# Eight instead of ten token blocks of MLP1 in front of the attention loop, and thirteen instead of seven MLP2 blocks in five stretches

## The chip, the cores and the metric

The kernel runs on one core of a Trainium2 chip. The metric is device time of one execution in microseconds (us), as the median of several runs. TensorE (PE) does the matrix products, VectorE (DVE), ScalarE (ACT) and GpSimd (POOL) the elementwise work, and SyncE (SP) issues nearly all DMA transfers.

## What is computed

The reference mixes two branches over S = 2048 tokens of D = 640 channels with a gate for each token. Branch A is attention with 32 query heads of 20 channels and a single key and value head. Branch B is the token-mixing MLP of an MLP-Mixer: layer norm over channels, then two products along the token axis (2048 to F = 1728 and back) with a tanh-approximated gelu between them.

```python
g = _sigmoid((x * gate_w).sum(-1, keepdims=True))
a = _A_ref(x, A_wq, A_wk, A_wv, A_wo)
b = _B_ref(x, B_w1, B_b1, B_w2, B_b2)
return g * a + (1 - g) * b
...
scores = jnp.einsum("bhqd,bkd->bhqk", q, k) * (Dh ** -0.5)
p = _softmax(scores, axis=-1)
o = jnp.einsum("bhqk,bkd->bhqd", p, v)
...
h = _layernorm(x, axis=-1)
u = jnp.einsum("bsd,sf->bdf", h, w1) + b1
u = _gelu(u)
y = jnp.einsum("bdf,fs->bds", u, w2) + b2
```

All inputs are float32. The kernel keeps that accuracy by splitting numbers into a high and a low part and summing three products: high by high, high by low, low by high.

## The kernel before

**Stages.** The order of the instructions on every engine is written out by hand (a manual schedule). There are five stages: (1) layer norm, transposes and the q, k, v projections; (2) a stage in front of the loop, in which TensorE computes blocks of MLP1 and starts on the row maxima; (3) the attention loop of 326 stretches, in which the rest of MLP1, all of MLP2 and part of the output projection are filled in between the scores; (4) a tail with the last attention units and output projections; (5) the last stores.

**Row tiles.** The score products contract over at most 62 rows, so two of them fit into the TensorE array one above the other. Each MLP product is cut into halves of 64 rows, and one half can run beside a score product in the other rows. In the loop, a stretch `k` works its scores in the rows of `b = k % 2` and its MLP matmuls in the other rows.

**Attention units.** There are 32 items (four query blocks of 512 by eight groups of four heads) of 16 key blocks, thus 512 units. A unit needs four score matmuls (L660), four exponentials (ScalarE, L663) and four matmuls with v (L687). The row maximum of the scores must be known before the exponentials, so all scores are computed once more, in another layout (L479), and reduced on VectorE (`tensor_reduce`, L482): 64 matmuls and reduces an item, 2048 in all. Of them, `LEAD = 48` pairs are done in stage 2, by `lead()`; the loop does six a stretch on average.

**MLP1.** A block is 128 of the 1728 hidden tokens for one half (320) of the channels; there are 14 blocks for each of two halves, 28 in all. A block has 16 steps of six matmuls: three products by two row halves. `PRO` of them, all of the first channel half, stand in stage 2 (L589), where both row halves run side by side into two banks, `pu0` and `pu1`. `pop_chain()` is called after each step and takes the next entry of the list `chain`, which holds the gelu of the block before: add the two banks (`add`, L525, VectorE), square (ScalarE), `cube` (L529, VectorE), `tanh` (ScalarE), `prod` (L535, VectorE), `high` (ScalarE), `low` (L541, GpSimd); `None` entries leave steps out. `cube_p`, `prod_p` (L548, L549) and `high_p` are the same on GpSimd, in two instructions each; the last block in front and the loop's blocks use them. In the loop a block takes six stretches of 16 matmuls.

**Lead.** In stage 2, the pairs of row-max matmuls are spread evenly over the steps from the fourth to the sixth before last. The matmuls take three PSUM banks in turn (`ps_m`), and a bank is free again when its reduce is done.

**Weights.** `w1_upto(n)` makes the high and low part of weight chunks up to chunk n: the high part (`wh`) on ScalarE for the first `4 * PRO` chunks and on GpSimd after that (L128), the low part (`wl`, L129) always on GpSimd. A block needs four chunks. SP's queue loads 256 KB for each, four chunks ahead.

**Query parts.** While `one_by_one` is set, the six transfers of a query tile are queued in `q_parts_due` and issued one at each quarter of a block, so that they don't crowd the weight loads. The queue must be empty before `fetch_max(0)` near the end of the stage.

**MLP2.** For each of 16 token blocks `st` and each channel half there are 81 matmuls of 64 rows. A block takes six stretches a channel half (13 or 14 matmuls each), or five (16 or 17). Five are possible because `twin_u` copies the first two hidden blocks to the other 64 rows, which evens out the two row halves over an odd number of stretches. `FIVE`, the number of blocks with five, is computed so that the loop has 326 stretches:

```python
FIVE = 6 * NS - (163 - 3 * (2 * FC - PRO) - 2 * NA)
```

With NS = 16, FC = 14, NA = 10 and PRO = 10 this is 7.

**A stretch.** `main(k, vs)` merges two lists by assumed times: the scores and row maxima in one row half, the MLP matmuls (and one or two row maxima) in the other. With more than 15 MLP matmuls it takes the pattern MANY (six scores, six row maxima), otherwise one of FEW (six scores with seven or five row maxima in turn). At the end of the MLP matmuls stands `signal()`, a tiny VectorE memset of `flag` (L673), so that a profile shows one `flag` for each stretch.

Of the kernel before, what the change touches and what calls it, by code (L numbers as in the profile page):

```python
# [12 lines left out]
ALU = mybir.AluOpType  # L13
# [12 lines left out]
NQB = S // NB  # L26
NQ = H // 4
NU = NQB * NQ
PRO = 10
LEAD = 48  # L30
TAIL = 24
BLOCKS = (2,) * 12
# [7 lines left out]
def mix_kernel(ctx: ExitStack, tc: tile.TileContext, A_x, A_wq, A_wk, A_wv, A_wo,  # L40
               B_x, B_w1, B_b1, B_w2, B_b2, gate_w, out):
    nc = tc.nc
# [3 lines left out]
    def f32(ap):  # L46
        return ap.bitcast(F32)
# [70 lines left out]
    def w1_upto(n):  # L118
        while fetched[0] < min(n, len(chunks)):
            c = fetched[0]  # L120
            w1_load(c + 1)
            wr = w1raw[c]
            wh = w1p.tile([P, HS, P], F32R, name="wh")
            wl = w1p.tile([P, HS, P], F32R, name="wl")
            if c < 4 * PRO:
                nc.scalar.activation(wh, wr, AF.Copy)  # L126
            else:
                nc.gpsimd.tensor_copy(wh, wr)  # L128
            nc.gpsimd.tensor_sub(wl, wr, f32(wh))  # L129
            w1t[c] = wh, wl  # L130
            fetched[0] += 1
            w1_load(c + 4)
# [20 lines left out]
    one_by_one, q_parts_due = [False], []  # L153

    def new_q(n):
        if n < NU:
            qtiles[n] = load_q(n, "qst")
# [309 lines left out]
    def ms_next(b):  # L467
        k = given[b]
        if k >= 32 * NU:
            return None  # L470
        given[b] += 1
        n, r = divmod(k, 32)
        (kq, pr), qt = divmod(r // 4, 2), r % 4

        def step():
            if n not in mtiles:
                mtiles[n] = mpool.tile([P, 16, 4], F32, name="mp")
            ms = next_bank()
            nc.tensor.matmul(ms, qmax[n][64 * b:64 * b + 60, pr, qt * P:(qt + 1) * P],  # L479
                             kst[64 * b:64 * b + 60, kq * NB:(kq + 1) * NB], start=True, stop=True)  # L480
            c = (2 * b + pr) * 4 + qt
            nc.vector.tensor_reduce(mtiles[n][:, c, kq:kq + 1], ms, axis=AX.X, op=ALU.max)  # L482
            issued[b] += 1
            if min(issued) == 32 * n + 1:
                new_qmax(n + 1)

        return step

    def ms_done():
        n = len(row_max)  # L490
        if n < NU and min(issued) >= 32 * (n + 1):
            mm = mmpool.tile([P, 16], F32, name="mm")
            nc.vector.tensor_reduce(mm, mtiles.pop(n), axis=AX.X, op=ALU.max)
            mn = mmpool.tile([P, 2, 16], F32R, name="mn")
            nc.gpsimd.tensor_scalar(mm, mm, -1.0, None, op0=ALU.mult)
            nc.gpsimd.tensor_copy(mn[:, 0, :], mm)
            nc.gpsimd.tensor_sub(mn[:, 1, :], mm, f32(mn[:, 0, :]))
            row_max[n] = mn

    def store_max(n):  # L500
        mn = row_max[n]
        mt = mpool.tile([P, 32], F32, name="mt")
        nc.vector.transpose(mt, f32(mn).rearrange("p j c -> p (j c)"))
        nc.sync.dma_start(out=m_scr[n], in_=mt)

    def fetch_max(n):
        src = m_scr[n].rearrange("(i j b r) e -> j b r i e", j=2, b=2, r=8)
        for b in range(2):
            for j in range(2):
                rows = f32(qtiles[n][64 * b + 60 + j:64 * b + 61 + j])  # L510
                nc.sync.dma_start(out=rows.rearrange("o p (t i e) -> o (p t) i e", i=4, e=32), in_=src[j, b][None])

    chain = []

    def gelu(d, fc, accs):
        both = fin.tile([P, D], F32, name="yo")
        xg, t1 = both[:, :HD2], both[:, HD2:]
        hi, lo = u_hi[d][:, fc, :], u_lo[d][:, fc, :]
        nc.scalar.activation(xg, accs[0][:, :HD2], AF.Identity, bias=bias[:, NS + fc:NS + fc + 1])

        def square():
            nc.scalar.activation(t1, xg, AF.Square)

        def add():
            nc.vector.tensor_add(xg, xg, accs[1][:, :HD2])  # L525
            square()

        def cube():
            nc.vector.scalar_tensor_tensor(t1, t1, 1.0 / 0.044715, xg, op0=ALU.add, op1=ALU.mult)  # L529

        def tanh():
            nc.scalar.activation(t1, t1, AF.Tanh, scale=GC * 0.044715)

        def prod():
            nc.vector.scalar_tensor_tensor(t1, t1, 1.0, xg, op0=ALU.add, op1=ALU.mult)  # L535

        def high():
            nc.scalar.activation(hi, t1, AF.Copy)

        def low():  # L540
            nc.gpsimd.tensor_sub(lo, t1, f32(hi))  # L541

        def cube_p():
            nc.gpsimd.tensor_scalar(t1, t1, 1.0, 1.0 / 0.044715, op0=ALU.mult, op1=ALU.add)
            nc.gpsimd.tensor_mul(t1, t1, xg)

        def prod_p():
            nc.gpsimd.tensor_scalar(t1, t1, 1.0, 1.0, op0=ALU.mult, op1=ALU.add)  # L548
            nc.gpsimd.tensor_mul(t1, t1, xg)  # L549

        def high_p():
            nc.gpsimd.tensor_copy(hi, t1)
            nc.gpsimd.tensor_sub(lo, t1, f32(hi))

        if len(accs) == 2 and fc == PRO - 1:
            add()
            chain.extend((cube_p, None, tanh, prod_p, high_p))
        elif len(accs) == 2:
            chain.extend((None, None, add, None, None, cube, tanh, None, prod, high, None, low))
        else:  # L560
            chain.extend((square, cube_p, None, tanh, prod_p, high_p))

    def pop_chain():
        f = chain.pop(0) if chain else None
        if f:
            f()

    with tc.tile_pool(name="psb", bufs=2, space=PSUM, side="right") as psb:
        at, skip, last = 0, 3, NS * PRO - 6
        one_by_one[0] = True  # L570

        def lead():
            for b in range(2):
                ms_next(b)()
            ms_done()

        for fc in range(PRO):
            pu = [psb.tile([P, NB], F32, name=f"pu{r}") for r in range(2)]
            for hf in range(4):
                w1_upto(4 * fc + hf + 4)  # L580
                if fc and q_parts_due:
                    q_parts_due.pop(0)()
                wh, wl = w1t.pop(4 * fc + hf)
                for c in range(HS):
                    st = hf * HS + c
                    for k, (w, h) in enumerate(((wh, h_hi[0]), (wh, h_lo[0]), (wl, h_hi[0]))):
                        for r in range(2):
                            rows = slice(64 * r, 64 * r + 64)
                            nc.tensor.matmul(pu[r][:, :HD2], w[rows, c, :], h[rows, st, :],  # L589
                                             start=(st == 0 and k == 0), stop=(st == NS - 1 and k == 2))  # L590
                    done = [max(0, min(x, last) - skip) * LEAD // (last - skip) for x in (at, at + 1)]
                    if done[1] > done[0]:
                        lead()
                    at += 1
                    pop_chain()
                if fc == 1 and hf == 0:
                    new_q(0)
                if fc == PRO - 2 and hf == 2:
                    assert not q_parts_due
                    one_by_one[0] = False  # L600
                    fetch_max(0)
            gelu(0, fc, pu)
            if fc == PRO - 3:
                store_max(0)
# [198 lines left out]
    def room(i):  # L803
        t, at = (u0, slot[0])[i % 8 // 4], 3 * D * (i % 4)
        return (t[:, at:at + 2 * D].rearrange("p (j c q) -> p j c q", j=2, q=P), f32(t[:, at + 2 * D:at + 3 * D]))
# [303 lines left out]
    for c in range(CUT // P, DC):  # L1109
        r = min(P, HEAD - c * P)  # L1110
        for st in held:
            oT, _ = room(len(jobs) - 4 + st - (NS - 4))
# [12 lines left out]
    for i in range(4):  # L1125
        st = NS - 4 + i
        for d in range(2):
# [7 lines left out]
            if (i, d) in ((0, 0), (1, 0), (2, 1), (3, 0), (3, 1)):  # L1135
                nc.vector.scalar_tensor_tensor(at[:, :HD2], acc[:, :HD2], g_col[:, st:st + 1], parts[st][:, sl],
                                               op0=ALU.mult, op1=ALU.add)
# [29 lines left out]
```

## Time and profile before

| what | us |
|---|---|
| median of 3 runs | 1677.76 (1677.33 to 1678.45) |
| profiled execution, its own time | 1677.69 |
| its span, first to last instruction | 1675.9 |
| first matmul of the blocks in front of the loop (L589) | at 96.1 |
| last matmul of these blocks | at 179.8 |
| first flag of the loop | at 183.2 |
| last flag of the loop | at 1596.4 |

The granted TensorE clock is 1.000 for the span. The stages differ in what keeps each engine busy:

| stretch of the span | length | DVE busy | ACT busy | POOL busy |
|---|---|---|---|---|
| MLP1 in the loop, 210 to 650 | 440 | 398.18 | 336.06 | 226.50 |
| MLP2 in five stretches, 650 to 957 | 307 | 276.79 | 224.69 | 82.68 |
| MLP2 in six stretches, 957 to 1423 | 466 | 418.85 | 346.03 | 105.58 |
| output projection, 1423 to 1597 | 174 | 156.81 | 133.69 | 33.35 |
| tail, 1597 to 1676 | 79 | 25.43 | 48.96 | 5.59 |

How to read the rows quoted below. A row of a group or line gives line, engine, operation, tiles written and read, count, and times in us, with durations of one instruction in ns. A row in order of time has its start, its length, and in square brackets how long the engine sat idle before it and whose work ended that; several instructions of a kind that follow each other closely are one row with their count. TensorE counts as busy almost everywhere, since matmuls overlap in the pipeline, so its pace is read from the starts of matmuls and not from its busy time.

### The profile page before, as it was taken

To read this page: it belongs to the slowest core of one execution; us is meant where nothing else is said; L and a number is where in the kernel's file an instruction comes from. 1 tells how busy PE (TensorE), PEld (TensorE's weight loads), DVE (VectorE), ACT (ScalarE), POOL (GpSimd) and SP (SyncE) were. 2 spreads that over 40 slices of the span, in tenths; PEclk is the share of its full clock that TensorE was granted. 3 is DMA by queue.
4 is the path that set the end of the run, shared out by engine and by line. 5 is a ranking of instruction groups with operands and counts; after the bars stand their busy time and mean duration, and the time that the engine had idled before them with its cause. 6 is when DMAs were issued, how large, how long until landed. Compare 5 with 4: busy or idle time off the path is not lost.

```text
span 1675.9 us, 38869 instructions
## 1 busy us (share of the span) xinstructions
PE 1668.3 (100%) x14865; PEld 1102.7 (66%) x14865; DVE 1440.1 (86%) x2745; ACT 1193.4 (71%) x2356; POOL 588.4 (35%) x727
## 2 busy tenths in 40 slices
PE   9999999999999999999999999999999999999998
PEld 7899766666666666666666656656665655666665
DVE  6679889989999998898989899899899989988933
ACT  4444677777777777777777777777777777777775
POOL 6568555555555543222323222122122220112210
PEclk9999999999999999999999999999999999999999
DMA  7665322222232321223212212122121221333611
GB/s 210 204 179 148 88 70 73 75 77 73 64 76 60 85 68 48 67 74 81 66 57 67 70 49 66 42 67 61 40 78 56 59 60 38 103 107 110 192 51 40
DMA packets 178304, 138.20 MB, mean 82 GB/s; under 512 B 33305, under 2 KB 144054, under 8 KB 178118
## 3 DMA queue, kind: packets, MB, share of 16 engines
q1 hardware_dynamic: 177830, 135.39, 29.3%
q8 instruction: 117, 1.92, 0.5%
q14 instruction: 69, 0.57, 0.1%
q10 hardware_dynamic: 288, 0.33, 0.1%
HBM read 102.36 MB, written 31.65 MB: 80 GB/s over the span
## 4 chain that ended last, share of the span: by engine, by line
PE 95%; issue 2%; DVE 1%; SPq 1%; ACT 0%; DMA 0%; POOL 0%; POOLq 0%; DVEq 0%; ACTq 0%
PE o L687 28%; PE ms L479 15%; PE s L660 12%; PE g L753 10%; PE ms L660 7%; PE g L932 6%; PE s L479 5%; PE pp L298 4%; PE pu L589 3%; PE g L878 2%; DVE mp L482 1%; PE ms L834 0%; PE pt L290 0%; ACT p L663 0%; SPq L195 0%
## 5 line engine op out<-in xcount | busy, mean ns | idle before, releaser
L482 DVE TENSOR_REDUCE mp<-ms 128x1 f32<-128x512 f32 x1298 | 839.3, 685 | 122.3 <-PE ms L479 97.8
L663 ACT ACTIVATE p<-s 128x512 f32<-128x512 f32 x1296 | 714.8, 607 | 241.0 <-PE s L660 205.5
L479 PE MATMUL ms<-kst,qmx 60*128 60x512 f32 x1298 | 552.4, 433 | 0.7 <-DVE mp L482 0.5
L660 PE MATMUL s<-qst,kst 62*128 62x512 f32 x1296 | 524.3, 410 | 0.0
L482 DVE TENSOR_REDUCE mp<-s 128x1 f32<-128x512 f32 x750 | 493.2, 682 | 23.3 <-PE s L479 23.0
L687 PE MATMUL o<-p,v_sb 128*32 128x512 f32 x4096 | 511.4, 601 | 0.0
L663 ACT ACTIVATE p<-ms 128x512 f32<-128x512 f32 x752 | 420.7, 602 | 112.3 <-PE ms L660 96.5
L479 PEld LDWEIGHTS ms<-kst,qmx 60*128 60x128 f32 x1298 | 238.3, 185 | 181.4 <-ACT p L663 91.3
L479 PE MATMUL s<-kst,qmx 60*128 60x512 f32 x750 | 311.8, 429 | 0.4 <-DVE yo L525 0.4
L660 PE MATMUL ms<-qst,kst 62*128 62x512 f32 x752 | 308.6, 410 | 0.0
L660 PEld LDWEIGHTS s<-qst,kst 62*128 62x128 f32 x1296 | 238.0, 186 | 92.4 <-DVE flag L673 62.0
L932 PE MATMUL g<-slot,wh 64*128 64x320 f32 x1152 | 268.0, 312 | 0.0
L129 POOL TENSOR_TENSOR wl<-wr,wh 128x512 fp32r<-128x512 f32 x176 | 230.5, 1312 | 42.9 <-ACT wh L126 21.7
L687 PEld LDWEIGHTS o<-p,v_sb 128*32 128x32 f32 x4096 | 97.6, 109 | 184.7 <-issue 176.9
L753 PE MATMUL g<-slot,wh 64*128 64x320 f32 x864 | 205.1, 313 | 0.0
L753 PE MATMUL g<-u,wh 64*128 64x320 f32 x864 | 205.0, 313 | 0.0
L932 PEld LDWEIGHTS g<-slot,wh 64*128 64x128 f32 x1152 | 190.7, 184 | 2.0 <-issue 1.7
L660 PEld LDWEIGHTS ms<-qst,kst 62*128 62x128 f32 x752 | 139.3, 185 | 66.1 <-issue 44.4
L932 PE MATMUL g<-slot,wl 64*128 64x320 f32 x576 | 179.9, 312 | 0.0
L709 POOL TENSOR_TENSOR ot<-ot,rl 128x512 f32<-128x512 f32 x30 | 31.5, 1051 | 361.0 <-DVE rl L708 361.0
L128 POOL CAST wh<-wr 128x512 fp32r<-128x512 f32 x136 | 83.4, 613 | 187.6 <-PE g L753 67.4
L753 PEld LDWEIGHTS g<-slot,wh 64*128 64x128 f32 x864 | 145.1, 184 | 2.4 <-ACT yo L761 2.1
(203 smaller groups left out, 2210.1 us busy)
## 6 DMA issues: line engine op xcount, KB each, us to landing
wr<-in_B_w_dram SPq DMA_DIRECT2D x152, 256.0 KB
qmx<-q_scr SPq DMA_DIRECT2D x192, 80.0 KB
qst<-q_scr SPq DMA_DIRECT2D x192, 80.0 KB
slot<-o_scr SPq DMA_DIRECT2D x20, 320.0 KB
y_scr<-yo SPq DMA_DIRECT2D x16, 320.0 KB
o_scr<-oh SPq DMA_DIRECT2D x124, 40.0 KB
o_scr<-ol SPq DMA_DIRECT2D x124, 40.0 KB
q_scr<-qh SPq DMA_DIRECT2D x19, 256.0 KB
```

The lines of the kernel that those rows point to most:

```text
L128: nc.gpsimd.tensor_copy(wh, wr)
L129: nc.gpsimd.tensor_sub(wl, wr, f32(wh))
L298: nc.tensor.matmul(pp, w, t, start=first and n == 0, stop=not more and n == len(steps) - 1)
L479: nc.tensor.matmul(ms, qmax[n][64 * b:64 * b + 60, pr, qt * P:(qt + 1) * P], kst[64 * b:64 * b + 60, kq * NB:(kq + 1) * NB], start=True, s ...
L482: nc.vector.tensor_reduce(mtiles[n][:, c, kq:kq + 1], ms, axis=AX.X, op=ALU.max)
L589: nc.tensor.matmul(pu[r][:, :HD2], w[rows, c, :], h[rows, st, :], start=(st == 0 and k == 0), stop=(st == NS - 1 and k == 2))
L660: nc.tensor.matmul(s, kst[64 * b:64 * b + 62, kb * P:(kb + 1) * P], q[64 * b:64 * b + 62, pr, :], start=True, stop=True)
L663: nc.scalar.activation(p, s, AF.Exp, scale=SCALE)
L687: nc.tensor.matmul(o[32 * hh:32 * hh + 32, :], v_sb[:, kb, :], ptiles.pop((u, hh)), start=(kb == 0), stop=(kb == NS - 1), skip_group_check ...
L753: other_tile(half, nc.tensor.matmul(hold["p"][:, :HD2], w[r, fc % HS, :], u[d][r, fc, :], start=(hold["n"] == 1), stop=(hold["n"] == 6 * F ...
L878: other_tile(half, nc.tensor.matmul(hold["p"][:, :HD2], o[r, c, :], w[r, c, d * HD2:(d + 1) * HD2], start=(hold["n"] == 1), stop=(hold["n" ...
L932: other_tile(half, nc.tensor.matmul(hold["p"][:, :HD2], w[r, st % HS, :], h[d][r, st, :], start=(hold["n"] == 1), stop=(hold["n"] == 6 * NS)))
```

## The change

`PRO` goes from 10 to 8, so blocks 8 and 9 of MLP1's first channel half leave the stage in front of the loop and become the first two blocks of the loop. `LEAD` stays at 48. `FIVE` follows from `PRO`: 96 - (163 - 60 - 20) = 13, so blocks 7 to 12 of MLP2 change from six to five stretches per channel half. The loop stays at 326 stretches, and the attention units and row maxima stay at the same stretch numbers: stretches 108 to 119 change from five-stretch MLP2 to MLP1, and stretches 178 to 249 from six-stretch to five-stretch MLP2.

In the blocks in front, the gelu's product moves from VectorE (one instruction) to GpSimd (two), the cube comes one step earlier, tanh and product follow one step earlier than before, and the high and low part two steps later than before (after steps 12 and 14 of the next block instead of 10 and 12). From block five on, the query parts are issued two at each quarter of a block instead of one.

```diff
-PRO = 10
+PRO = 8
...
-        def prod():
-            nc.vector.scalar_tensor_tensor(t1, t1, 1.0, xg, op0=ALU.add, op1=ALU.mult)
-
...
-            chain.extend((None, None, add, None, None, cube, tanh, None, prod, high, None, low))
+            chain.extend((None, None, add, None, cube, tanh, None, prod_p, None, None, None, high, None, low))
...
-                if fc and q_parts_due:
-                    q_parts_due.pop(0)()
+                for f in [q_parts_due.pop(0) for _ in range(min(len(q_parts_due), 1 + fc // 5))] if fc else []:
+                    f()
```

The function that the new chain calls stands in both kernels:

```python
def prod_p():
    nc.gpsimd.tensor_scalar(t1, t1, 1.0, 1.0, op0=ALU.mult, op1=ALU.add)
    nc.gpsimd.tensor_mul(t1, t1, xg)
```

## The prediction

> **What bounds the kernel now.** I read the page first, then the busy time of each engine in single stretches, then the instructions of two stages in order of time, since the shares of the whole span mix stages with different limits.
>
> ```profile
> span 1675.9 us, 38869 instructions
> PE 1668.3 (100%) x14865; PEld 1102.7 (66%) x14865; DVE 1440.1 (86%) x2745; ACT 1193.4 (71%) x2356; POOL 588.4 (35%) x727
> PE 95%; issue 2%; DVE 1%; SPq 1%; ACT 0%; DMA 0%; POOL 0%; POOLq 0%; DVEq 0%; ACTq 0%
> ```
>
> The chain that ended last is TensorE almost throughout, with VectorE close behind it. The change moves work between two stages, so each needs a price of its own. The first is the block stage in front of the loop, the ten token blocks of L589:
>
> ```profile
> L589 PE MATMUL pu<-slot,wh x640: 302/306/417, 96.1 to 179.7; 64*128 64x320 f32 x160
> L589 PE MATMUL pu<-slot,wl x320: 300/306/307, 96.6 to 179.8; 64*128 64x320 f32 x160
> 96.15:179.80 83.65, 83.00 (x1057) 81.51 (x1057) 76.14 (x132) 37.26 (x73) 62.62 (x53) 1.00 0.58 159
> ```
>
> The third row has the stretch, then busy time (and instructions) of PE, PEld, DVE, ACT and POOL, the granted clock, the DMA share and GB/s. The stage takes 83.65 us, 8.4 a block; VectorE is busy for 76.1 of it, GpSimd for 62.6. How the two leaders mesh is seen in order of time, TensorE first, then VectorE:
>
> ```profile
> 98.90 0.45 PE L589 MATMUL pu<-slot,wh 64*128 64x320 f32 x4
> 99.19 0.31 PE L589 MATMUL pu<-slot,wl 64*128 64x320 f32 x2
> 99.34 0.39 PE L479 MATMUL ms<-kst,qmx 60*128 60x512 f32 x2
> 99.57 0.46 PE L589 MATMUL pu<-slot,wh 64*128 64x320 f32 x4
> 99.86 0.31 PE L589 MATMUL pu<-slot,wl 64*128 64x320 f32 x2
> 100.01 0.45 PE L589 MATMUL pu<-slot,wh 64*128 64x320 f32 x4
> ...
> 100.45 0.46 PE L589 MATMUL pu<-slot,wh 64*128 64x320 f32 x4
> ...
> 100.89 0.39 PE L479 MATMUL ms<-kst,qmx 60*128 60x512 f32 x2
> ```
>
> ```profile
> 99.77 1.29 DVE L482 TENSOR_REDUCE mp<-ms 128x1 f32<-128x512 f32 x2 [1.37 <-PE ms L479]
> ...
> 104.42 1.29 DVE L482 TENSOR_REDUCE mp<-ms 128x1 f32<-128x512 f32 x2 [0.26 <-PE ms L479]
> 105.98 1.29 DVE L482 TENSOR_REDUCE mp<-ms 128x1 f32<-128x512 f32 x2 [0.26 <-PE ms L479]
> 107.19 0.48 DVE L525 TENSOR_TENSOR yo<-yo,pu 128x320 f32<-128x320 f32 x1
> 107.58 1.28 DVE L482 TENSOR_REDUCE mp<-ms 128x1 f32<-128x512 f32 x2
> ...
> 117.66 0.48 DVE L529 SCALAR_TENSOR_TENSOR yo<-yo 128x320 f32<-128x320 f32 x1
> 118.06 1.28 DVE L482 TENSOR_REDUCE mp<-ms 128x1 f32<-128x512 f32 x2
> 119.26 0.48 DVE L535 SCALAR_TENSOR_TENSOR yo<-yo 128x320 f32<-128x320 f32 x1
> 119.65 1.28 DVE L482 TENSOR_REDUCE mp<-ms 128x1 f32<-128x512 f32 x2
> ```
>
> A step of a block is six matmuls of L589: 0.44 us (99.57 to 100.01). A pair of row-max matmuls adds 0.23 (99.34 to 99.57). Here a pair comes every three steps: 3 x 0.44 + 0.23 = 1.55, which is 99.34 to 100.89. VectorE needs 1.21 us a pair (105.98 to 107.19) and so stands idle 0.27 before most: TensorE sets the pace. The add (L525), the cube (L529) and the product (L535) of a gelu take 0.40 each of VectorE's order (107.19 to 107.58, 117.66 to 118.06, 119.26 to 119.65).
>
> The second is the loop. VectorE sets a flag at the end of each of its 326 stretches, so a window that holds n flags is n stretches long. These three windows lie in the MLP1, the five-stretch MLP2 and the six-stretch MLP2 part (length, flags' busy time and their count, clock, DMA share, GB/s):
>
> ```profile
> 231.93:649.25 417.32, 5.66 (x96) 1.00 0.28 72
> 692.43:957.21 264.78, 3.54 (x60) 1.00 0.25 67
> 957.21:1423.36 466.15, 6.37 (x108) 1.00 0.21 57
> ```
>
> A stretch takes 417.32 / 96 = 4.347 us with 16 MLP1 matmuls beside the scores, 264.78 / 60 = 4.413 with 16 or 17 MLP2 matmuls, 466.15 / 108 = 4.316 with 13 or 14. The number of stretches, the score matmuls, exponentials and row-max reduces per two stretches are the same in all three.
>
> **The change part by part.** *The loop.* It stays at 326 stretches. Blocks 8 and 9 of the first MLP1 half enter it with 12 stretches. The number of five-stretch blocks, computed from PRO, goes from 7 to 13, and that shortens MLP2 by 6 x 2 = 12. By place in the loop, 12 stretches turn from five-stretch MLP2 to MLP1, and 72 from six-stretch to five-stretch MLP2. The price is 72 x (4.413 - 4.316) = +7.0 and 12 x (4.347 - 4.413) = -0.8, so **+6.2 us**. With the 70 stretches of the old five-stretch part taken as a whole, its cheap first block included, it would come out about 1 us lower, so I keep +5.2 to +6.8.
>
> *Two blocks leave the stage in front.* That takes 2 x 16 steps of 0.44 us off TensorE, 14.1 us. The 48 row-max pairs stay, now over 128 steps instead of 160. TensorE alone would need 128 x 0.44 + 48 x 0.23 = 67.4 us; the same sum for before is 160 x 0.44 + 11.0 = 81.4, so 2.2 us of the measured 83.65 were stalls.
>
> *VectorE.* A pair of row maxima now comes every two or three steps, 119 / 48 = 2.48 on average: 2.48 x 0.44 + 0.23 = 1.32 us of TensorE, against 1.21 of VectorE for the reduces plus its gelu work. Before, that was an add for ten blocks and cube and product for nine; after, an add for eight and a cube for seven, since the last block's cube was on GpSimd already. VectorE's sum is 48 x 1.21 + 8 x 0.40 + 7 x 0.40 = 64.1 us after, 48 x 1.21 + 28 x 0.40 = 69.3 before. So its share rises from 69.3 / 81.4 = 85% to 64.1 / 67.4 = 95%, and the 0.27 of idle time that took in a late reduce is mostly gone. With three banks for row maxima, TensorE gets about one pair ahead and then waits, with the blocks' matmuls queued behind the row-max matmul. Add and cube come close together, 0.8 us in each block; three-step intervals win back 0.34, two-step ones (1.11 us) lose 0.10. I take half of the 0.8, 0.4 us a block, as TensorE stall: 3.2 us.
>
> *The product on GpSimd.* Nine products leave VectorE, two of which go with the blocks that leave. In their place GpSimd runs two instructions for each block that stays in front; the last block's were there already:
>
> ```profile
> L548 POOL TENSOR_SCALAR yo<-yo 128x320 f32<-128x320 f32 x19 | 8.7, 457 | 2.4 <-ACT yo L532 2.3
> L549 POOL TENSOR_TENSOR yo<-yo 128x320 f32<-128x320 f32 x19 | 16.6, 875 | 1.6
> L129 POOL TENSOR_TENSOR wl<-wr,wh 128x512 fp32r<-128x512 f32 x40 | 55.7, 1403 | 18.8 <-ACT wh L126 18.3
> L541 POOL TENSOR_TENSOR u<-yo,u 128x320 fp32r<-128x320 f32 x9 | 7.9, 875 | 1.9 <-ACT u L538 0.9 <-PE ms L479 0.9
> ```
>
> That is 1.33 us a block, on top of four weight splits of 1.40 and one low part of 0.88: 7.8 us a block. TensorE takes at least 67.4 / 8 = 8.4, so it is covered. The halves of u that the moved product yields are first read by the MLP2 blocks, hundreds of us later; behind the product on GpSimd wait the next weight splits, which are made four chunks ahead (4 x 83.65 / 40 = 8.4 us). So the later places of the high and low steps in the chain cost nothing. If that cover were gone, a block would cost what GpSimd needs (second rival).
>
> *Contention of VectorE and GpSimd.* Cube and product usually take 0.48 us, but some take much longer:
>
> ```profile
> L529 DVE SCALAR_TENSOR_TENSOR yo<-yo x9: 479/482/1291, 108.8 to 175.0; 128x320 f32<-128x320 f32 x9
> L535 DVE SCALAR_TENSOR_TENSOR yo<-yo x9: 475/480/1276, 109.8 to 177.5; 128x320 f32<-128x320 f32 x9
> ...
> L535 DVE SCALAR_TENSOR_TENSOR yo<-yo 128x320 f32<-128x320 f32 x9 | 6.2, 687 | 0.5 <-ACT yo L532 0.5
> L529 DVE SCALAR_TENSOR_TENSOR yo<-yo 128x320 f32<-128x320 f32 x9 | 5.9, 654 | 0.0
> ```
>
> The cubes took 654 ns on average for a median of 482, so 0.17 us too long each. Seven cubes give 1.2 us at that rate, and 7 x 0.81 = 5.7 if all took the longest. I take 1.2, the measured mean. The Trainium skill speaks against the change here (GPSIMD Engine Reference, Key points): GpSimd shares its SBUF interfaces with VectorE, and VectorE instructions with two SBUF inputs contend. The cube is one, and the spread of the rows agrees.
>
> *Queues.* The two blocks' weight loads (eight of 256 KB) move past the loop's start on SP's queue. The query parts are issued two at a time from block five on, so that they are out before the row maxima are fetched. The row of the stage in front shows the DMA engines at 0.58 of their time; after, 0.8 of its weights go in about 0.87 of its time, so the rate hardly changes. I cost it at nothing; a late part would be paid by the row-max pairs of the second item.
>
> *Sum.* The stage in front: 67.4 + 3.2 + 1.2, and 1.0 for stalls that stay (the old 2.2, less a good half: the nine products ran 0.21 us each over their median, 1.9 in all, and that is gone from VectorE): **72.8 us**, 10.9 less than 83.65. With the loop's +6.2, the kernel gets 4.7 us shorter. Around the span lie 1677.69 - 1675.9 = 1.8 us in the profiled execution, and its 1677.69 is 0.07 below the median of the runs, 1677.76. So 1677.7 - 4.7 = **1673.0 us**.
>
> **The rivals.**
>
> *TensorE's own pace.* One pair of lookahead suffices; the stage costs 67.4 plus the old 2.2, 69.6 us, and the whole 1677.7 - 14.0 + 6.2 = 1669.9. For it: VectorE's sum is still below TensorE's. Against: 5% of slack where 15% did not prevent 2.2 us of stalls. 18%.
>
> *GpSimd becomes the bound of the stage in front (the slower one).* Its queue is in order: a product that comes before its tanh is done holds the weight splits behind it, then TensorE lacks weights. The first group row of GpSimd shows 18.8 us of waiting in front of 40 splits, 1.9 a block. If that stays beside the 7.8 and the product waits 0.8 for its tanh, a block takes 10.5, the stage 84.0, and the time is 1677.7 + 0.35 + 6.2 = 1684.3. It is slower than before from (83.65 - 6.2) / 8 = 9.7 us a block on. Against: those waits are for ScalarE's cast, which waits until TensorE leaves a buffer; they are slack that shrinks when GpSimd has more to do. 8%.
>
> *Every cube meets GpSimd.* GpSimd is busy for 7.8 of about 9.1 us of a block, up from 62.62 / 83.65 = 75% to 86%. With 5.7 instead of 1.2 the stage costs 77.3, the saving is 6.4, and the time 1677.5: no change. The Trainium skill's rule, named above, would give this if each overlap were paid in full by VectorE. For it stand the maxima of 1.29, against it the medians at 0.48. 20%.
>
> *The loop's price is not paid*, because the six-stretch part is cheap for another reason than its fewer matmuls: 1677.7 - 10.9 = 1666.8. Against it, the five- and six-stretch parts lie next to each other in the same loop and differ at once. 4%.
>
> **How the numbers follow.** The forecast as worked out, with 71 to 75 us in front and so about 1671 to 1675, has 50%. A measurement of this kernel cannot tell less than about 0.2%, 3.4 us, from no change: faster means below 1674.4. The first and the last rival (22%) and three quarters of the forecast (37%) lie there: 59%. The rest of the forecast and the cube rival make 33% for no change. 8% is left for slower. The range goes from 1669.5 (TensorE's own pace, less 0.4) to 1678.0 (every cube, and the loop at +6.8); it leaves out the loop rival and the GpSimd one.
>
> **What would show it.** In the changed kernel's profile L586 should span 71 to 75 us for eight blocks, with hardly an idle gap before VectorE's reduces, and TensorE waiting for them (row maxima released by a reduce). The flags should give about 4.41 us a stretch over 130 MLP2 stretches and 4.35 over the 120 of MLP1, with 36 left at 4.32. No product stands on VectorE; GpSimd's stage in front is 85 to 90% busy. I am wrong if TensorE waits for wh or wl there, if cubes at 1.2 us are the rule, or if the new five-stretch blocks cost what the six-stretch ones did per stretch.

## The result, and the profile after

| | median us | runs |
|---|---|---|
| before | 1678.11 | 6 (1677.33 to 1679.40) |
| changed | 1672.51 | 6 (1671.08 to 1674.18) |

The ratio is 0.9967, with a 95% interval of 0.9956 to 0.9977: 5.6 us faster, clear of no change, where 4.7 had been forecast. The profiled execution of the changed kernel has a span 6.2 us shorter than that of before. Its page begins:

```profile
span 1669.7 us, 38827 instructions
PE 1661.0 (99%) x14865; PEld 1105.5 (66%) x14865; DVE 1435.7 (86%) x2732; ACT 1188.0 (71%) x2346; POOL 606.3 (36%) x759
```

The matmuls of the blocks in front (L586 is L589 of before) by their first and last start, and the stage as one window (length, busy time and count of PE, PEld, DVE, ACT, POOL, then clock, DMA share, GB/s):

```profile
L586 PE MATMUL pu<-slot,wh x512: 301/305/418, 96.5 to 167.9; 64*128 64x320 f32 x171
L586 PE MATMUL pu<-slot,wl x256: 300/305/309, 96.9 to 168.1; 64*128 64x320 f32 x128
96.45:168.09 71.64, 69.92 (x866) 67.65 (x866) 67.05 (x119) 29.12 (x57) 57.03 (x58) 1.00 0.56 155
```

The stage takes 71.6 us instead of 83.65: **12.0 us saved**. VectorE is now busy for 67.05 of 71.64 us, 94% (91% before), GpSimd for 80% (75%). What VectorE's reduces waited for there (total, times, longest) was 6.2 us in 17 waits before:

```profile
DVE mp L482 <- PE ms L479: 6.2, 17, 1.4
```

and in the changed kernel:

```profile
DVE mp L482 <- PE ms L479: 1.8, 6, 0.9
```

A second profile of the changed kernel (`c0_changed`) gives somewhat more:

```profile
DVE mp L482 <- PE ms L479: 2.5, 10, 0.9
```

The other way round, TensorE's weight loads (PEld) and matmuls (PE) for the row maxima wait for reduces. In the stage before, then changed:

```profile
PEld ms L479 <- DVE mp L482: 1.8, 4, 0.7
PE ms L479 <- DVE mp L482: 0.5, 2, 0.4
```

```profile
PEld ms L479 <- DVE mp L482: 3.1, 5, 1.4
PE ms L479 <- DVE mp L482: 1.7, 4, 1.1
```

TensorE keeps VectorE waiting far less and VectorE keeps TensorE waiting more: the two have come about level. The flags of the changed loop, all 326, then its MLP1, five-stretch and six-stretch parts as windows with the count of flags:

```profile
L670 DVE MEMSET flag<- x326: 59/59/59, 171.5 to 1590.1; 1x1 f32 x163
```

```profile
220.30:688.29 467.99, 6.37 (x108) 1.00 0.27 71
732.23:1261.33 529.10, 7.08 (x120) 1.00 0.23 65
1261.33:1416.88 155.55, 2.12 (x36) 1.00 0.20 57
```

From the first to the last flag it takes 1418.6 us instead of 1413.2: **5.4 us paid**. A stretch takes 467.99 / 108 = 4.333 us in MLP1, 529.10 / 120 = 4.409 in five-stretch and 155.55 / 36 = 4.321 in six-stretch MLP2, within 0.02 us of the same kinds before. In the second profile of the changed kernel the flags lie 1419.2 us apart, so there about 6 us are paid. The stages before the first block and after the last flag moved by less than 0.5 us.

### The profile page after: what moved, and what is told of

Same layout as the page of the kernel before. It is cut to its first block, busy times and chain, and to the rows that moved or that the text cites. A ratio compares the mean times of both kernels' runs of the same rounds, so it can differ in the third digit from the quotient of the medians.

```text
span 1669.7 us, 38827 instructions
## 1 busy us (share of the span) xinstructions
PE 1661.0 (99%) x14865; PEld 1105.5 (66%) x14865; DVE 1435.7 (86%) x2732; ACT 1188.0 (71%) x2346; POOL 606.3 (36%) x759
## 4 chain that ended last, share of the span: by engine, by line
PE 95%; issue 2%; DVE 1%; SPq 1%; ACT 0%; DMA 0%; POOL 0%; POOLq 0%; DVEq 0%; ACTq 0%
PE o L684 28%; PE ms L479 18%; PE s L657 13%; PE g L750 10%; PE g L929 7%; PE ms L657 5%; PE pp L298 4%; PE s L479 3%; PE pu L586 3%; PE g L875 2%; DVE mp L482 1%; PE ms L831 0%; ACT p L660 0%; PE pt L290 0%; SPq L195 0%
## 5 line engine op out<-in xcount | busy, mean ns | idle before, releaser
L482 DVE TENSOR_REDUCE mp<-ms 128x1 f32<-128x512 f32 x1514 | 967.2, 685 | 130.2 <-PE ms L479 102.7
L660 ACT ACTIVATE p<-s 128x512 f32<-128x512 f32 x1512 | 820.6, 606 | 299.4 <-PE s L657 280.2
L479 PE MATMUL ms<-kst,qmx 60*128 60x512 f32 x1514 | 646.5, 433 | 1.7 <-DVE mp L482 1.7
L657 PE MATMUL s<-qst,kst 62*128 62x512 f32 x1512 | 601.6, 403 | 0.0
L479 PEld LDWEIGHTS ms<-kst,qmx 60*128 60x128 f32 x1514 | 279.0, 184 | 244.9 <-ACT p L660 114.7
L482 DVE TENSOR_REDUCE mp<-s 128x1 f32<-128x512 f32 x534 | 355.6, 683 | 12.0 <-PE s L479 11.8
L660 ACT ACTIVATE p<-ms 128x512 f32<-128x512 f32 x536 | 305.1, 599 | 56.8 <-PE ms L657 50.2
L479 PE MATMUL s<-kst,qmx 60*128 60x512 f32 x534 | 230.8, 441 | 0.4 <-DVE yo L525 0.4
L657 PE MATMUL ms<-qst,kst 62*128 62x512 f32 x536 | 216.8, 405 | 0.0
L750 PEld LDWEIGHTS g<-u,wh 64*128 64x128 f32 x864 | 143.5, 184 | 1.1 <-issue 1.1
```

What stands on the lines that cost most here:

```text
L657: nc.tensor.matmul(s, kst[64 * b:64 * b + 62, kb * P:(kb + 1) * P], q[64 * b:64 * b + 62, pr, :], start=True, stop=True)
L660: nc.scalar.activation(p, s, AF.Exp, scale=SCALE)
L750: other_tile(half, nc.tensor.matmul(hold["p"][:, :HD2], w[r, fc % HS, :], u[d][r, fc, :], start=(hold["n"] == 1), stop=(hold["n"] == 6 * F ...
```

## The experiments

The runs were made in three groups, each with the kernel before beside it: the changed kernel once more with the two runs of the moved product and the fourth bank (before took 1677.82 us); seven and nine blocks and the two pattern runs (1677.68); ten blocks with the fourth bank and the three late cubes (1677.93). The ratios are to before of the same group.

| run | blocks in front | stage in front, us | median us | ratio to before (95%) |
|---|---|---|---|---|
| before | 10 | 83.7 | 1677.7 to 1677.9 | 1 |
| changed (`c0_changed`) | 8 | 71.7 | 1672.00 | 0.9964 (0.9951 to 0.9976) |
| product on VectorE | 8 | 73.2 | 1673.80 | 0.9976 (0.9967 to 0.9986) |
| ten blocks, product on GpSimd | 10 | 83.5 | 1678.00 | 1.0001 (0.9992 to 1.0010) |
| fourth bank | 8 | 69.5 | 1669.71 | 0.9950 (0.9938 to 0.9963) |
| ten blocks, fourth bank | 10 | 81.7 | 1675.79 | 0.9987 (0.9978 to 0.9996) |
| nine blocks | 9 | 76.6 | 1673.54 | 0.9975 (0.9965 to 0.9984) |
| seven blocks | 7 | 69.5 | 1672.56 | 0.9965 (0.9952 to 0.9979) |
| FEW everywhere | 8 | 71.6 | 1696.47 | 1.0113 (1.0099 to 1.0127) |
| MANY everywhere | 8 | 71.6 | 1680.21 | 1.0016 (1.0008 to 1.0025) |
| late cube | 8 | 73.2 | 1673.05 | 0.9972 (0.9962 to 0.9982) |
| late cube, fourth bank | 8 | 69.8 | 1674.24 | 0.9979 (0.9970 to 0.9988) |
| ten blocks, GpSimd product, late cube | 10 | 85.3 | 1683.37 | 1.0034 (1.0021 to 1.0047) |

The stage is measured from its first to its last matmul start in each profile.

**The changed kernel as control.**

> The changed kernel itself, beside the others of this comparison. Ratio to before 0.9967 again (0.9956 to 0.9977); the blocks in front of the loop take 71 to 72 us from their first to their last matmul, the 326 flags lie 1418 to 1419 us apart from first to last.

It came out as expected, 0.9964 and 71.7 us in front, but for the flags: they lie 1419.2 us apart, just above the range.

**Is it VectorE or TensorE that sets the stage now?** The first run puts the product back on VectorE in the changed kernel:

```diff
-chain.extend((None, None, add, None, cube, tanh, None, prod_p, None, None, None, high, None, low))
+chain.extend((None, None, add, None, cube, tanh, None, prod, None, None, None, high, None, low))
```

> The changed kernel with the gelu product of the eight blocks on VectorE again, one instruction at the same place of the chain. If VectorE's order sets the stage in front once eight blocks stand there, seven products add 7 x 0.40 = 2.8 us, and 1.5 more if they run 0.21 over their median as before: the stage 74.4 to 75.9 us instead of 71.6, the kernel 2.8 to 4.3 us slower than the changed one. If TensorE's own pace sets it, nothing: the stage at most 72.1.

Within this group the runs do not overlap with the changed kernel's, 1673.80 against 1672.00; the six runs of the result, though, reach up to 1674.18, so the firmer evidence is the stage, 1.5 to 1.6 us longer than in the two profiles of the changed kernel. So VectorE's work counts, but the run misses its range: 73.2 us against 74.4 to 75.9. The 1.5 us for contention did not come, since both SBUF instructions were quick here; why the 2.8 us of work show as 1.5 was not settled:

```profile
L529 DVE SCALAR_TENSOR_TENSOR yo<-yo 128x320 f32<-128x320 f32 x7 | 3.6, 519 | 0.5 <-ACT yo L522 0.5
L535 DVE SCALAR_TENSOR_TENSOR yo<-yo 128x320 f32<-128x320 f32 x7 | 3.4, 486 | 0.0
```

Fewer and more blocks in front vary the balance (`PRO = 7`, `PRO = 9`; the five-stretch blocks follow):

> PRO = 7: one block more moves into the loop, and all sixteen MLP2 blocks take five stretches. If VectorE's order sets the stage in front at eight blocks already, one add and one cube less save 0.8 us there: 70.5 to 71.3 us instead of 71.6. The loop pays 30 stretches from six- to five-stretch MLP2 at 0.097 and 6 to MLP1 at 0.031, +3.1: the kernel 2 to 3 us slower than the changed one. If TensorE's work sets the stage: 7 us less there (64.5), the kernel 4 us faster.

> PRO = 9, ten MLP2 blocks in five stretches. TensorE's sum is 144 x 0.44 + 11.0 = 74.4 us, VectorE's 64.9: TensorE sets the pace again, with 1 to 3 us of stalls, 75.4 to 77.4 in front. The loop gives back 3.1. The kernel 0.7 to 2.7 us slower than the changed one. If each block were worth the same from ten to eight, it would lie in the middle, 2.8 slower.

Their stages, seven blocks first, then nine:

```profile
L586 PE MATMUL pu<-slot,wh x448: 301/305/418, 96.9 to 166.2; 64*128 64x320 f32 x150
L586 PE MATMUL pu<-slot,wl x224: 300/305/309, 97.3 to 166.4; 64*128 64x320 f32 x112
```

```profile
L586 PE MATMUL pu<-slot,wh x576: 301/306/417, 96.5 to 172.9; 64*128 64x320 f32 x192
L586 PE MATMUL pu<-slot,wl x288: 300/306/307, 96.9 to 173.1; 64*128 64x320 f32 x144
```

From the kernel before to nine blocks the stage falls by 7.1 us (6.9 from ten blocks with the same chain, the 83.5 below), which is about a block's whole TensorE time of 16 x 0.44 = 7.0; from nine to eight by 4.9; from eight to seven by 2.2. TensorE sets the stage above eight blocks, VectorE below, and at eight they share it. The nine-block run came within its range. The seven-block one missed: 2.2 us saved, not 0.8, and no loss of 2 to 3 us in the kernel, whose ratio cannot be told from the changed kernel's. The loop did pay about what was forecast: its flags lie 1421.7 us apart, against 1418.6 and 1419.2. At seven blocks VectorE's reduces wait for TensorE only once, 0.9 us, in place of 1.8:

```profile
DVE mp L482 <- PE ms L479: 0.9, 1, 0.9
```

I had counted the work that VectorE loses and not the idle time that goes with it. I missed by 1.4 us; these waits fell by 0.9 against the first profile of the changed kernel and by 1.6 against the second.

**Does the moved product pay by itself?** The kernel before, ten blocks, with the changed kernel's chain:

> The kernel before with ten blocks in front, but with the changed kernel's chain, product on GpSimd. With ten blocks TensorE sets the pace and only its 2.2 us of stalls can go: the stage 82.0 to 82.9 us instead of 83.65, the kernel 0.7 to 1.6 us faster than before. If the moved product were the larger part of the gain: 4 us or more. If GpSimd's contention eats it: no gain or a loss.

Nothing: 1.0001, and the stage is 83.5 us. VectorE has nine products less and TensorE is stalled as long as before. The cube in that run (its first line gives count and min/median/max in ns):

```profile
L529 DVE SCALAR_TENSOR_TENSOR yo<-yo x9: 485/491/979, 108.3 to 175.4; 128x320 f32<-128x320 f32 x9
its engine sat idle before it (us, times) until:
  ACT yo L522: 2.2, 4
```

It stands one step earlier, so in four blocks it follows the add with no reduce between them and holds VectorE until ScalarE has made the square. So the run moves the cube too and does not test the product alone. That the product on VectorE makes none of the stalls at ten blocks is shown by the fourth bank below. Taken with the 1.8 us that the product costs on VectorE at eight blocks, it is worth something where VectorE is the bound, and nothing that these runs show where TensorE is.

**Where do the stalls come from?** A fourth PSUM bank for the row maxima in front (the bank of the loop's MLP matmuls, idle there):

```diff
+front = [0]
 ...
         if not ring:
+            front[0] += 1
+            if front[0] % 4 == 0:
+                return ps_g.tile([P, NB], F32, name="g")
             return ps_m.tile([P, NB], F32, name="ms")
```

> The changed kernel with a fourth PSUM bank for the row maxima in front of the loop (the bank that the loop's MLP matmuls use later, idle there). If TensorE's stalls of 4.2 us come from a lookahead of about one pair, two pairs of lookahead take a good part: the stage 69 to 70.5 us, the kernel 1 to 2.5 us faster than the changed one. If VectorE's sum sets the stage whatever the lookahead: 71.0 to 71.8 and no difference over 0.6 us.

> The kernel before, ten blocks, with the fourth bank for the row maxima in front. If the bank helps because TensorE and VectorE stand close to each other at eight blocks (the changed kernel gained 2.3 us by it), it is worth less here, where TensorE leads by 12 us: at most the 2.2 us of stalls, some 0.5 to 1.5. If the bank is worth the same whatever the balance, 2 us or more.

Both gain: 2.3 us over the changed kernel, 2.1 over before. The second was expected to be smaller; the bank is worth the same at both balances. At ten blocks the stage of 81.7 us, with the product on VectorE, is within 0.3 of TensorE's own sum of 81.4: the stalls were lookahead, also those that I had put down to the product. At eight, VectorE in order of time shows what is left (reduces into `g` are those of the fourth bank):

```profile
131.08 1.29 DVE L486 TENSOR_REDUCE mp<-ms 128x1 f32<-128x512 f32 x2
132.27 0.48 DVE L529 TENSOR_TENSOR yo<-yo,pu 128x320 f32<-128x320 f32 x1
132.66 0.69 DVE L486 TENSOR_REDUCE mp<-ms 128x1 f32<-128x512 f32 x1
133.26 0.69 DVE L486 TENSOR_REDUCE mp<-g 128x1 f32<-128x512 f32 x1
133.86 0.49 DVE L533 SCALAR_TENSOR_TENSOR yo<-yo 128x320 f32<-128x320 f32 x1
134.26 1.89 DVE L486 TENSOR_REDUCE mp<-ms 128x1 f32<-128x512 f32 x3
```

No idle time stands in brackets: a reduce starts 0.60 us after the last, add and cube take 0.40 each. VectorE's order is full here; over the whole stage its reduces still wait 1.5 us for TensorE, in four places. This kernel, 0.9950 (0.9938 to 0.9963), beats both.

**Is it the count of matmuls that makes a five-stretch block's stretch dearer?** In the changed kernel, one pattern of scores and row maxima for all stretches:

```diff
-            sx, sf = (MANY if len(fs) > 15 else FEW)[len(vs) == 1]
+            sx, sf = FEW[len(vs) == 1]
```

and the other way round with MANY.

> The changed kernel with the order of the 13-matmul stretches (six scores and seven or five row maxima in turn, pattern FEW) in all stretches. If the fuller stretches cost more because of their order of scores and maxima (their pattern MANY), 250 of them get up to 0.097 us cheaper, 24 us in all. If the 2.7 more matmuls beside the scores are the cost, nothing is won, or some is lost.

> The changed kernel with the pattern MANY (six scores, six row maxima) in all stretches, so also in the 36 of six-stretch MLP2 and the 40 of the output projection. If the pattern is what costs 0.097 us a stretch, these get dearer by 76 x 0.097 = 7.4 us at most, and a six-stretch one takes 4.41. If the count of matmuls is the cost, they stay at 4.32 and the kernel within 1 us of the changed one.

Neither theory holds. With FEW, the MLP1 and the five-stretch part get dearer, 428.05 / 96 = 4.459 and 539.80 / 120 = 4.498 us:

```profile
274.78:702.83 428.05, 5.66 (x96) 1.00 0.27 70
747.51:1287.31 539.80, 7.08 (x120) 1.00 0.23 63
1287.31:1442.29 154.98, 2.12 (x36) 1.00 0.20 57
```

The third row is the six-stretch part, whose pattern stays: 154.98 / 36 = 4.305. With MANY, the five-stretch part stays at 529.26 / 120 = 4.411, and the six-stretch part takes 163.26 / 36 = 4.535, more than the 4.41 that was expected if the pattern were the cost:

```profile
731.83:1261.09 529.26, 7.08 (x120) 1.00 0.24 65
1261.09:1424.35 163.26, 2.12 (x36) 1.00 0.19 55
```

Under one pattern, MANY, a stretch with *fewer* matmuls is the dearer one (4.535 against 4.411); under FEW it is the cheaper (4.305 against 4.498). Each kind needs its own pattern, and 0.09 us is the difference between two pairs of kind and pattern, not a price of 2.7 matmuls. What in the patterns makes it was not settled.

**What is the cube's earlier place worth?** Cube, tanh and product one step later, in the changed kernel, with the fourth bank, and with ten blocks and three banks:

```diff
-chain.extend((None, None, add, None, cube, tanh, None, prod_p, None, None, None, high, None, low))
+chain.extend((None, None, add, None, None, cube, tanh, None, prod_p, None, None, high, None, low))
```

> The changed kernel with cube, tanh and product one step later, where they stood before. In the last block the cube then no longer follows the add at once, so VectorE doesn't wait 0.54 us for the square and TensorE's stall of 1.44 us there goes: the stage 70.2 to 71.0 us instead of 71.6, the kernel 0.6 to 1.4 us faster than the changed one. If the earlier cube is worth something elsewhere: no gain, or a loss.

> Both: fourth bank and the cube one step later. VectorE's order sets the stage throughout with four banks (reduces 0.60 us apart); the wait of 0.54 and the cube of 1.31 us in the last block go: the stage 67.8 to 69.0 us instead of 69.5, the kernel 1668.2 to 1669.2. If the last block's end is set by something else: 69.5 and 1669.7 as with four banks alone.

> The kernel before, ten blocks, with the product on GpSimd but the cube at its old place. If the run with ten blocks and the new chain won nothing because the earlier cube waited for its square (2.2 us in four blocks), this one has the gain of the moved product: the stage 82.0 to 82.9 us, the kernel 0.7 to 1.6 us faster than before. If the product is worth nothing at ten blocks in any place, 0.

All three went the wrong way. In the first the stage is 1.5 us longer than the changed kernel's (the medians, 1673.05 and 1672.00, come from two groups of runs, and their intervals overlap). What changed is the cube; the changed kernel, then the late cube:

```profile
L529 DVE SCALAR_TENSOR_TENSOR yo<-yo x7: 478/479/775, 109.0 to 162.6; 128x320 f32<-128x320 f32 x7
```

```profile
L529 DVE SCALAR_TENSOR_TENSOR yo<-yo x7: 480/936/1310, 109.5 to 165.4; 128x320 f32<-128x320 f32 x7
```

The median goes from 479 to 936 ns, and the seven cubes take 2.2 us more in all. That fits the 1.5 us but does not fix them: with the fourth bank the late cubes are as slow (6.4 us in all against 4.2), and the stage grows by only 0.3. At ten blocks most late cubes stay quick (a median of 480 ns). In order of time, a weight split of GpSimd and a cube of VectorE, first in the changed kernel:

```profile
115.30 1.30 POOL L129 TENSOR_TENSOR wl<-wr,wh 128x512 fp32r<-128x512 f32 x1
117.18 1.65 POOL L129 TENSOR_TENSOR wl<-wr,wh 128x512 fp32r<-128x512 f32 x1 [0.58 <-ACT wh L126]
```

```profile
117.19 0.48 DVE L529 SCALAR_TENSOR_TENSOR yo<-yo 128x320 f32<-128x320 f32 x1
```

and then with the late cube:

```profile
135.44 2.56 POOL L129 TENSOR_TENSOR wl<-wr,wh 128x512 fp32r<-128x512 f32 x2
```

```profile
137.41 0.94 DVE L529 SCALAR_TENSOR_TENSOR yo<-yo 128x320 f32<-128x320 f32 x1
```

Started together, the cube passes and the split takes 1.65 us instead of 1.30. Started while a split runs, the cube lasts until 138.35, 0.35 after the splits' end at 138.00.

The other two runs lose 4.5 and 5.4 us against the same kernel with the early cube, most of it between the last block and the loop. In the run with the fourth bank, the first flag of the loop comes 8.1 us after the last block's last matmul (173.9 - 165.8), with ten blocks 6.8 (188.1 - 181.3), in the changed kernel 3.4. Who waited for whom at that place with the fourth bank:

```profile
ACT u L539 <- POOL yo L550: 4.6, 1, 4.6
DVE yo L529 <- ACT yo L523: 3.7, 1, 3.7
PE s L483 <- DVE yo L529: 3.2, 1, 3.2
```

and GpSimd's order there:

```profile
163.52 0.87 POOL L128 CAST wh<-wr 128x512 fp32r<-128x512 f32 x1
164.47 1.29 POOL L129 TENSOR_TENSOR wl<-wr,wh 128x512 fp32r<-128x512 f32 x1
165.71 0.60 POOL L128 CAST wh<-wr 128x512 fp32r<-128x512 f32 x1
166.39 1.28 POOL L129 TENSOR_TENSOR wl<-wr,wh 128x512 fp32r<-128x512 f32 x1
167.62 0.48 POOL L549 TENSOR_SCALAR yo<-yo 128x320 f32<-128x320 f32 x1
168.18 0.86 POOL L550 TENSOR_TENSOR yo<-yo 128x320 f32<-128x320 f32 x1
```

With the early cube (fourth bank) the same place is:

```profile
158.94 0.61 POOL L128 CAST wh<-wr 128x512 fp32r<-128x512 f32 x1
159.63 1.29 POOL L129 TENSOR_TENSOR wl<-wr,wh 128x512 fp32r<-128x512 f32 x1
161.86 0.46 POOL L549 TENSOR_SCALAR yo<-yo 128x320 f32<-128x320 f32 x1 [0.94 <-DVE mp L486]
```

There the product comes after one cast and split, and GpSimd stands idle for 0.94 us before it. With the late cube the product (the last two rows of the longer list) has fallen behind one cast and split more, 1.9 us (165.71 to 167.62), and the queue itself runs late. Over the stage ScalarE's high parts wait 23.4 us for products, against 10.8 with the early cube, and the casts that GpSimd's next splits need stand behind them on ScalarE (a high part at 159.13, the cast at 159.50, the split at 160.20); how much of the 4.5 us each of the two makes was not separated. At the end, ScalarE's high part waits for the product, the next gelu's first step stands behind that on ScalarE, VectorE's add waits for that step, and the loop's first row-max matmul waits for the add to free its PSUM bank.

## Why the prediction was right, and where not

- **TensorE's floor, 14.1 us less work in front.** Right. The stage kept 12.0 of them; 10.9 were forecast.
- **VectorE comes to 95% and holds TensorE back.** Right in kind: the reduces' waits fell from 6.2 us to 1.8 and 2.5 in the two profiles, the product back on VectorE makes the stage 1.5 us longer, and the step from eight to seven blocks saves 2.2 us where the one from ten to nine saves 6.9 to 7.1. The rival of TensorE's own pace (69.6 us in front) fell; with a fourth bank the stage comes to 69.5, but there VectorE's order is nearly full. The 95% was too low where it counts. It compares sums over the whole stage, but the pairs stand in 119 of the 128 steps, and the last block's add starts behind the stage (at 169.0). For these steps TensorE needs 119 x 0.44 + 11.0 = 63.4 us, VectorE 48 x 1.21 + 7 x 0.40 + 7 x 0.40 = 63.7: by this estimate the two are level, with no slack.
- **3.2 us of stalls for add and cube, 1.0 for old stalls that stay.** The sum of 67.4 + 4.2 = 71.6 is the measured stage to the tenth, and that is luck: some contention is in it too, and its split was wrong. I had put a good half of the old 2.2 us down to the product. Without the product on VectorE the ten-block stage still takes 83.5 us, and with a fourth bank and the product still there 81.7: it was lookahead.
- **1.2 us of contention on the cubes.** The mis-sized term of the stage. I took the old rate, but the cube comes at another place now. In the changed kernel the median is 479 ns and one of seven was slow (775), so contention cost VectorE about 0.3 us. One step later, at eight blocks, the rate would have been higher, not lower: a median of 936.
- **GpSimd's extra work is covered.** Right for the changed kernel: the stage spent no wait of TensorE on GpSimd's weight splits. GpSimd was busy for 80% of the stage, not the 85 to 90% forecast: the 7.8 us a block were counted for eight blocks, but only 31 splits, seven products and six low parts lie in the window, and a split took 1.36 us, not 1.40. The cover is thin: cube, tanh and product one step later cost 4.5 us with four banks. The GpSimd rival had the right queue (a product behind splits) at the wrong place: the victim was not the weights but the hand-over of the banks to the loop.
- **+6.2 us in the loop.** Measured +5.4 and about +6 in the two profiles, inside the bounds of 5.2 to 6.8. Five-stretch MLP2 came at 4.409 us against 4.413 forecast. The prices were right as measured prices of kind and pattern; my reading, that the count of matmuls makes them, did not survive the two pattern runs.

In the first profile the stage came out 1.2 us shorter than forecast, 0.9 of it by the contention, and the loop 0.8 cheaper; some 0.4 were given back ahead of the first block and behind the last flag, so the forecast of 4.7 fell 1.5 short of the profiled 6.2. In the second profile the loop is close to its forecast and the span 5.7 us shorter than before. The changed issue of the query parts, costed at nothing, was not varied by itself; from the last matmul in front to the first flag it takes 3.4 us before and after.

## What to carry to other kernels

Price a stage by the engine that comes second as well: taking work off the first pays in full only until the two are level. Another buffer between them can be worth as much as more work moved, and here it was so on both sides of that point (2.1 and 2.3 us for one idle bank). In an order written by hand, the place of a cheap instruction can be worth more than the instruction: one step decided whether most cubes took 0.48 or 0.94 us, and whether a product stood before or behind another cast and split of an in-order queue. A stage's measured price per step can be carried to new steps of the same kind without knowing its cause, but the cause then still has to be tested.

## What the hardware showed

VectorE's two-input instructions on SBUF and GpSimd's two-input weight splits exclude each other rather than share. The one that comes later waits until the other is done: a cube that met a running split ended 0.35 us after it (137.41 + 0.94 against 138.00), and a split that started within 0.02 us of a cube took 1.65 us instead of 1.30. The 14 traces hold 32 cubes and products that started 0.3 to 1.05 us after a split and before its last 0.2 us; all of them ended 0.35 us after it. Of the 75 that started at most 0.02 us after a split, 74 passed and the split grew to 1.63 to 1.66 us; one, in the run with seven blocks, waited itself and took 1.62. The Trainium skill (GPSIMD Engine Reference, Key points) tells of contention on the shared SBUF interfaces for such VectorE instructions; the runs agree and show its size here, the rest of the other engine's instruction. The reduces from PSUM kept their 0.60 us beside running splits.
